# One 256-column lane and then 512 columns in the first block of a fused attention and two-layer kernel, with part of the weight scaling moved to ScalarE

## The chip, the cores and the metric

The kernel runs on one NeuronCore of a Trainium2 chip. The metric is the device time of the whole program in microseconds (us), lower is better. Engines are named as in the profile: PE is TensorE (PEld its weight loads), DVE is VectorE, ACT is ScalarE, SP is SyncE, which here only issues DMAs.

## The reference

Three stages run one after the other on fp32 data; the output of each feeds the next.

```python
s = concat([scale * q_l @ k_g.T, where(|i-j| <= 32, scale * q_l @ k_l.T, -1e9)])   # local rows
out_l = softmax(s) @ concat([v_g, v_l]);  out_g = softmax(scale * q_g @ k_all.T) @ v_all
x  = concat([out_g, out_l]) as 2176 rows x 512
h  = x @ w_in;  g = max(h, 0) + alpha * min(h, 0);  x = g @ w_out                  # layer 1, 512 -> 2048 -> 512
h  = x @ w_in2; x = (h * clip(h + 3, 0, 6) / 6) @ w_out2                            # layer 2
```

## The kernel before, in words

**Layer 1** goes over five blocks of rows (`blocks`; the first three of 512 rows, which are the columns of every matmul here). Within a block the hidden width of 2048 is cut into `NJ` = 16 chunks `j` of 128. A step computes one chunk: `h_tile` (L424) makes the chunk of h in 12 matmuls (4 chunks of the model width, three products each, since a fp32 number is split into a high and a low part), `act` applies the activation (ACT `t` L434, DVE `t` L436, ACT `g` L442, DVE `g` L443), and `LAG` = 2 steps later `y_tiles` (L455) adds g times the second weight to the four sums y, in 12 matmuls.

**The first block** needs its weights and its x while both are still being made. x comes from the local attention (`attention_steps`; scores L194, softmax L212 and L216, transposes L227, values L240), two steps of which are interleaved with each of the first four steps, and one with each later step. Four later attention steps make one pair of units. Since only the first 256 rows are there when the block starts, it has two lanes: columns 0 to 256 run chunk j at step s = j, columns 256 to 512 run chunk j at step s = j + `DELAY`, with `DELAY` = 4. So steps 0 to 3 have 12 h matmuls of 256 columns, steps 4 to 15 have 24 of them (two chunks, 256 columns each), steps 16 to 19 have 12. Before step 4 the x of the second lane is transposed (L409) and split (ACT L395, DVE L396).

**The weights** arrive as raw 64-bit words, one half chunk (128x512) at a time: a DMA (`load_raw`, L94) into one of `RAW` = 5 buffers, then `to_float32`: ACT clamps the low word in place (L109), DVE scales the high word into a tile z of `ZB` = 2 buffers (L113), DVE shifts and merges (L117), DVE merges the sign (L119). `split_w` then makes the high part on ACT (L125) and the low part on DVE (L126). There are 32 halves. The class `Weights` converts them in the order in which the steps need them: `needed(s)` counts the halves that steps up to s use, and step s converts as far as step s + `AHEAD` = 2 needs. All this is in program order for the clamp and the scaling (`here`); the rest of the order is set by a scheduler that simulates the program.

Blocks 1 to 4 use the converted weights, with 512 columns (384 and less in the last two). The weights of layer 2 are converted with the same `to_float32` during blocks 1 to 4. Layer 2 follows.

Of the kernel before, what the change touches and what calls it, by code (L numbers as in the profile page):

```python
# [12 lines left out]
U32 = mybir.dt.uint32  # L13
# [9 lines left out]
NJ = DFF // 128  # L23
# [7 lines left out]
LAG = 2  # L31
RAW = 5
EARLY = 3
AHEAD = 2
# [5 lines left out]
TB = 2  # L40
DELAY = 4
STEPS = [[2] * 4 + [1] * 16, [1] * 16, [1] * 16, [1] * 16, [0] * 16]
CONVERT = (3, 4, 5)
SPLIT = (0, 70, 70, 30, 43)
STREAM = 3
# [10 lines left out]
def fused_kernel(ctx, tc, qkE, vE, qgz, kN, vN, vgN, w1, w2, consts, out):  # L56
# [41 lines left out]

    here = tc.keep_in_program_order

    def to_float32(raw, on_dve=True):

        words = raw.bitcast(U32).rearrange("p (f two) -> p f two", two=2)
        low, high = words[:, :, 0], words[:, :, 1]
        here(nc.scalar.activation(low, low, AF.Relu, bias=quarter_sb, scale=0.9 * 2.0 ** -29))  # L109
        z = work.tile([128, 512], F32, tag="z", name="z", bufs=ZB)  # L110
        bits = z.bitcast(U32)
        if on_dve:
            here(nc.vector.tensor_scalar(out=z, in0=high.bitcast(F32), scalar1=2.0 ** -112, scalar2=None,  # L113
                                         op0=ALU.mult))
        else:
            here(nc.scalar.activation(z, high.bitcast(F32), AF.Copy, scale=2.0 ** -112))
        nc.vector.scalar_tensor_tensor(out=bits, in0=bits, scalar=3, in1=low, op0=ALU.logical_shift_left,  # L117
                                       op1=ALU.bitwise_or)
        nc.vector.scalar_tensor_tensor(out=bits, in0=high, scalar=0x80000000, in1=bits, op0=ALU.bitwise_and,  # L119
                                       op1=ALU.bitwise_or)  # L120
        return z

    def split_w(raw, wt, m):
        z = to_float32(raw)
        nc.scalar.copy(wt[:, m, 0, :], z)  # L125
        nc.vector.tensor_tensor(out=wt[:, m, 1, :], in0=z, in1=wt[:, m, 0, :].bitcast(F32), op=ALU.subtract)  # L126

    class Weights:
# [1 line left out]


        def __init__(self, src, early=False):
            self.src, self.raw, self.next, self.wt, self.got = src, {}, 0, {}, 0
            self.seq = [(j, m) for j in range(NJ) for m in range(2)]
            if early:
                self.seq.sort(key=lambda h: (h[0] + LAG * h[1], -h[1]))
# [5 lines left out]
        def fetch(self, upto):  # L142
            while self.got < min(upto, 2 * NJ):
                self.raw[self.got] = load_raw(self.src, *self.seq[self.got])
                self.got += 1

        def convert(self, halves):
            for _ in range(halves):
                k = self.next
                if k == 2 * NJ:  # L150
                    return
                self.fetch(EARLY)
                j, m = self.seq[k]
                if j not in self.wt:
                    self.wt[j] = wp.tile([128, 2, 2, 512], F32R, tag="w", name="wt", bufs=NJ)
                split_w(self.raw.pop(k), self.wt[j], m)
                self.fetch(k + EARLY + 1)
                self.next += 1

# [231 lines left out]
    width = [sum(128 if x == "g" else 256 for x in blk) for blk in blocks]  # L391
# [6 lines left out]
    def x_tiles():  # L398
        return [work.tile([128, 2, 512], F32R, tag="xt", name="xt", bufs=HP) for _ in range(HP)]

    def x_from_attention(pieces, xt, at):

        for hp in range(HP):
            t = bank("xt_ps")
            n = 0
            for piece in pieces:
                x = xo.pop(("g", hp) if piece == "g" else (*piece, hp))
                for i in range(1 if piece == "g" else 2):
                    nc.tensor.transpose(t[:, n:n + 128], x if piece == "g" else x[:, i, :], ident_sb)  # L409
                    n += 128  # L410
            split_x(t[:, :n], xt[hp][:, :, at:at + n], n)

    def active(lanes, s):
        return [(a, b, s - d) for a, b, d in lanes if 0 <= s - d < NJ]

    def h_tile(xt, wts, parts):
        ps = bank("h_ps")
# [26 lines left out]
    def y_tiles(layer, y, g, wts, parts, lanes=False):  # L446
        for a, b, j in parts:
            steps = [(w, c) for w in ((0, 0), (1, 0), (0, 1)) for c in range(len(y))]
            if j == NJ - 1:
                steps.sort(key=lambda step: step[1])  # L450
            for (wl, gl), c in steps:
                first = a == 0 and j == 0 and (wl, gl) == (0, 0)
                last = j == NJ - 1 and (wl, gl) == (0, 1) and (not lanes or b == 512)
                if layer == 0:
                    nc.tensor.matmul(y[c][:, a:b], lhsT=wts[j][:, 1, wl, 128 * c:128 * c + 128], rhs=g[:, gl, a:b],  # L455
                                     start=first, stop=last, skip_group_check=lanes)
                else:
                    nc.tensor.matmul(y[c], lhsT=g[:, gl, 128 * c:128 * c + 128], rhs=wts[j][:, 1, wl, :],
                                     start=first, stop=last)
# [22 lines left out]
    def attention_steps(n):  # L482

        for _ in range(n):
            if state["gen"] is None:
                return
            try:
                next(state["gen"])
            except StopIteration:
                state["pool"].close()  # L490
                state["gen"] = None
                if not state.get("global"):
                    state["global"] = True
                    state["pool"] = ExitStack()
                    state["gen"] = global_units(state["pool"].enter_context(tc.tile_pool(name="gatt", bufs=1)))

    def ready(pieces):
        return all((("g", hp) if x == "g" else (*x, hp)) in xo for x in pieces for hp in range(HP))
# [438 lines left out]
    W1 = Weights(w1, early=True)  # L937
# [5 lines left out]
    k = 0  # L943
    while not ready(blocks[0][:1]):
        attention_steps(1)
        k += 1
        if k in CONVERT:
            W1.convert(1)
# [3 lines left out]
    for bi in range(len(blocks)):  # L952
        n = width[bi]
        last = bi == len(blocks) - 1
        lanes = [(0, 256, 0), (256, 512, DELAY)] if bi == 0 else [(0, n, 0)]
        y = [psy.tile([128, 512], F32, tag="y", name="y_ps", bufs=4) for _ in range(NC)]
        gs, xt_next = {}, None
        end = NJ + lanes[-1][2]
        for s in range(end + LAG):
            if s < end:  # L960
                if bi == 0:
                    if s == DELAY:
                        while not ready(blocks[0][1:]):
                            attention_steps(1)
                        x_from_attention(blocks[0][1:], xt, 256)
                    W1.convert(W1.needed(s) - W1.next)
                    W1.convert(min(1, W1.needed(s + AHEAD) - W1.next))
                parts = active(lanes, s)
                gs[s] = act(0, h_tile(xt, W1.wt, parts), parts)
                if bi == 0:  # L970
                    W1.convert(W1.needed(s + AHEAD) - W1.next)
                attention_steps(STEPS[bi][s])
            if last and s == 0:
                while state["gen"] is not None:
                    attention_steps(1)
                outs_pool.close()
                later["xs"] = pool("xs")
                more = inputs(twos[0], bt)
                plan_stream()
            if s == end - 1 and not last:  # L980
                xt_next = x_tiles()
                while not ready(blocks[bi + 1]):
                    attention_steps(1)
                x_from_attention(blocks[bi + 1], xt_next, 0)
            if s >= LAG:
                y_tiles(0, y, gs.pop(s - LAG), W1.wt, active(lanes, s - LAG), len(lanes) > 1)
            done = [SPLIT[bi] * max(x - REST, 0) // (end + LAG - REST) for x in (s, s + 1)]
            for _ in range(done[1] - done[0]):
                next(second, None)
            if last and s >= 2:  # L990
                next(more, None)
        if last:
            for _ in second:
                pass
            for _ in more:
                pass
            ahead(STREAM + RAW - 2)
        for c in range(0, NC, 2):
            r = work.tile([128, 2, 512], F32, tag="g", name="ev", bufs=LAG + 1)[:, :, :n]
            nc.scalar.copy(r[:, 0, :], y[c][:, :n])  # L1000
            nc.vector.tensor_copy(r[:, 1, :], y[c + 1][:, :n])
            for i in range(2):
                nc.sync.dma_start(out=x2[bi][:, c + i, :], in_=r[:, i, :])
        xt = xt_next
# [64 lines left out]
```

## Time and profile before

| | |
|---|---|
| median of 3 runs | 840.43 us (839.70 to 842.15) |
| profiled execution, its own time | 838.92 us |
| span in the profile of that execution | 836.8 us |
| PE busy | 817.8 us (98%), 7228 matmuls |
| PEld busy | 740.3 us (88%) |
| DVE busy | 594.1 us (71%) |
| ACT busy | 415.4 us (50%) |
| granted TensorE clock, mean | 0.994 of full speed |

The profiled execution took 2.1 us more than the span, and 1.5 us less than the median of the runs. A busy PE here is PE with a matmul in its pipeline; how fast the matmuls follow each other is read from where they start. A row of a timeline gives start, duration, engine, line, tensors and count; the duration contains a tail that overlaps the next instruction.

### The profile page before, as it was taken

The numbers are of one execution on the slowest core, as the hardware profiler recorded it, in microseconds if no ns is written. First come the engines' busy times: TensorE is split into PE (matmuls) and PEld (weight loads), VectorE is DVE, ScalarE is ACT, GpSimd is POOL, SyncE is SP. The second block draws the span as 40 slices with busy tenths as digits, with TensorE's granted clock in tenths as the row PEclk, the third lists the DMA queues.
The fourth block names the chain that finished last, engine by engine and source line by source line (L and its number), as shares of the span: only waits on it lengthen the run. The fifth ranks groups of instructions, "written<-read, shape, count | busy, mean of one in ns | idle before, by whom it ended". The sixth has DMA issues, their size and how long they took to land.

```text
span 836.8 us, 18274 instructions
## 1 busy us (share of the span) xinstructions
PE 817.8 (98%) x7228; PEld 740.3 (88%) x7228; DVE 594.1 (71%) x1319; ACT 415.4 (50%) x905; POOL 0.2 (0%) x4
## 2 busy tenths in 40 slices
PE   6889999999999999989999999999999999999997
PEld 4779999888888888878899988889999999999996
DVE  4999995477878786787678847778867678854221
ACT  5876665455656554455454523434543444432222
POOL 0000000000000000000000000000000000000000
PEclk9999999999999999999999999999999999999999
DMA  9976563367768876798575555666675878788872
GB/s 334 340 267 239 181 215 119 109 210 254 272 215 296 270 253 238 256 312 297 182 263 203 166 200 190 193 208 215 201 239 199 295 255 284 243 280 262 276 255 67
DMA packets 72868, 195.70 MB, mean 234 GB/s; under 512 B 7120, under 2 KB 18384, under 8 KB 72784
## 3 DMA queue, kind: packets, MB, share of 16 engines
q1 hardware_dynamic: 72688, 194.42, 68.8%
q8 instruction: 57, 0.93, 0.4%
q14 instruction: 27, 0.22, 0.1%
q10 hardware_dynamic: 96, 0.13, 0.1%
HBM read 152.05 MB, written 42.47 MB: 232 GB/s over the span
## 4 chain that ended last, share of the span: by engine, by line
PE 86%; DVE 6%; DMA 3%; ACT 3%; issue 1%; SPq 0%; DVEq 0%; ACTq 0%
PE y_ps L455 20%; PE h_ps L424 19%; PE o_ps L859 17%; PE k_ps L776 16%; PE h_ps L928 4%; PE o_ps L714 4%; DMA raw<-in_w 2%; PE o_ps L240 1%; PE s_ps L194 1%; DVE z L117 1%; PE pt_ps L227 1%; DVE z L119 1%; DVE wt L126 1%; DVE z L113 1%; PE xt_ps L409 1%
## 5 line engine op out<-in xcount | busy, mean ns | idle before, releaser
L455 PE MATMUL y_ps<-g,wt 128*128 128x256 f32 (+2 forms) x1152 | 209.3, 331 | 3.4 <-ACT g L442 1.7
L424 PE MATMUL h_ps<-xt,wt 128*128 128x256 f32 (+2 forms) x1152 | 206.3, 329 | 1.4 <-DVE xt L396 0.9
L455 PEld LDWEIGHTS y_ps<-g,wt 128*128 128x128 f32 x1152 | 176.5, 189 | 23.0 <-ACT g L442 2.1
L424 PEld LDWEIGHTS h_ps<-xt,wt 128*128 128x128 f32 x1152 | 177.8, 190 | 18.7 <-DVE xt L396 1.1
L859 PE MATMUL o_ps<-ws,gh 128*128 128x256 f32 x784 | 139.4, 283 | 0.0
L776 PE MATMUL k_ps<-bt,ws 128*128 128x512 f32 (+1 forms) x672 | 135.1, 362 | 0.0
L776 PEld LDWEIGHTS k_ps<-bt,ws 128*128 128x128 f32 x672 | 121.2, 188 | 13.0
L859 PEld LDWEIGHTS o_ps<-ws,gh 128*128 128x128 f32 x784 | 120.8, 192 | 0.1
L859 PE MATMUL o_ps<-ws,gl 128*128 128x256 f32 x392 | 107.0, 283 | 0.0
L790 DVE TENSOR_TENSOR gl<-far,gh 128x1024 fp32r<-128x1024 f32 (+1 forms) x56 | 60.9, 1089 | 33.0 <-ACT gh L789 32.7
L789 ACT CAST gh<-far 128x1024 fp32r<-128x1024 f32 (+1 forms) x56 | 52.7, 942 | 62.8 <-PE o_ps L859 58.5
L436 DVE SCALAR_TENSOR_TENSOR t<-t,c_sb,h_ps 128x256 f32<-128x256 f32 (+2 forms) x96 | 55.2, 588 | 32.3 <-ACT t L434 32.0
L859 PEld LDWEIGHTS o_ps<-ws,gl 128*128 128x128 f32 x392 | 73.5, 192 | 0.0
L434 ACT ACTIVATE t<-h_ps 128x512 f32<-128x512 f32 (+2 forms) x84 | 42.8, 511 | 52.9 <-PE h_ps L424 51.2
L442 ACT CAST g<-t 128x512 fp32r<-128x512 f32 (+2 forms) x84 | 45.3, 539 | 43.8 <-DVE t L436 43.7
L443 DVE TENSOR_TENSOR g<-t,g 128x512 fp32r<-128x512 f32 (+2 forms) x84 | 49.2, 587 | 21.3 <-ACT g L442 18.7
L761 ACT ACTIVATE t<-far,half_sb 128x512 f32<-128x512 f32 (+1 forms) x48 | 32.1, 671 | 50.9 <-DVE far L757 49.7
L216 ACT ACTIVATE p<-p,st 128x128 f32<-128x128 f32 x128 | 49.7, 390 | 11.9 <-DVE st L212 11.9
L109 ACT ACTIVATE raw<-raw,quarter_sb 128x512 uint32<-128x512 uint32 x64 | 49.6, 775 | 3.7 <-DMA raw<-in_w 3.7
L117 DVE SCALAR_TENSOR_TENSOR z<-z,raw 128x512 uint32<-128x512 uint32 x64 | 43.7, 691 | 3.3 <-ACT raw L109 0.8
L119 DVE SCALAR_TENSOR_TENSOR z<-raw,z 128x512 uint32<-128x512 uint32 x64 | 43.6, 689 | 0.7
L928 PE MATMUL h_ps<-xt,ws 128*128 128x384 f32 x192 | 36.0, 336 | 0.0
(100 smaller groups left out, 854.8 us busy)
## 6 DMA issues: line engine op xcount, KB each, us to landing
ws<-wo SPq DMA_DIRECT2D x72, 512.0 KB, 4.2
raw<-in_w SPq DMA_DIRECT2D x64, 512.0 KB, 5.4
ws<-wi SPq DMA_DIRECT2D x64, 512.0 KB, 4.6
v_t<-in_vE SPq DMA_DIRECT2D x32, 512.0 KB, 7.1
qk_t<-in_qkE SPq DMA_DIRECT2D x32, 368.0 KB, 5.5
wi<-raw SPq DMA_DIRECT2D x16, 512.0 KB, 3.1
wi<-parts SPq DMA_DIRECT2D x16, 512.0 KB, 4.5
wo<-raw SPq DMA_DIRECT2D x16, 512.0 KB, 4.0
```

What stands on the lines that cost most here:

```text
L109: here(nc.scalar.activation(low, low, AF.Relu, bias=quarter_sb, scale=0.9 * 2.0 ** -29))
L117: nc.vector.scalar_tensor_tensor(out=bits, in0=bits, scalar=3, in1=low, op0=ALU.logical_shift_left, op1=ALU.bitwise_or)
L119: nc.vector.scalar_tensor_tensor(out=bits, in0=high, scalar=0x80000000, in1=bits, op0=ALU.bitwise_and, op1=ALU.bitwise_or)
L216: nc.scalar.activation(p[:, n, :], p[:, n, :], AF.Exp, bias=st[:, 1, n:n + 1], scale=-1.0, accum_out=st[:, 2, n:n + 1])
L424: nc.tensor.matmul(ps[:, a:b], lhsT=wts[j][:, 0, wl, 128 * c:128 * c + 128], rhs=xt[c][:, xl, a:b], start=k == 0, stop=k == 3 * NC - 1)
L436: nc.vector.scalar_tensor_tensor(out=t[:, c:d], in0=t[:, c:d], scalar=c1_sb[:, j:j + 1], in1=ps[:, c:d], op0=ALU.mult, op1=ALU.add)
L455: nc.tensor.matmul(y[c][:, a:b], lhsT=wts[j][:, 1, wl, 128 * c:128 * c + 128], rhs=g[:, gl, a:b], start=first, stop=last, skip_group_check ...
L776: nc.tensor.matmul(bank, lhsT=wt[:, wl, at:at + 128], rhs=bt[x][:, c, xl, 0:w], start=first and k == 0, stop=k == 5, skip_group_check=True)
L789: nc.scalar.copy(hi, src)
L790: nc.vector.tensor_tensor(out=lo, in0=src, in1=hi.bitcast(F32), op=ALU.subtract)
L859: mm = nc.tensor.matmul(bank, lhsT=part[:, jp, 128 * c:128 * c + 128], rhs=wo[:, jp, 256 * wl:256 * wl + 256], start=opens, stop=k == NP / ...
L928: nc.tensor.matmul(h, lhsT=wt[:, wl, 128 * c:128 * c + 128], rhs=xt[c][:, xl, 0:w], start=k == 0, stop=k == 3 * NC - 1)
```

## The change

From the ninth half on (`SCALED_ON_DVE` = 8) the scaling of the high word runs on ACT, as `AF.Copy` with a scale, and `to_float32` is cut in two: `begin_float32` (load of the raw words, clamp, scaling) is called one half ahead of `end_float32` (the two merges). The first block keeps the 20 steps, but steps 0 to 3 run columns 0 to 256 for chunks 0 to 3, steps 4 to 7 run columns 256 to 512 for the same chunks 0 to 3, and steps 8 to 19 run all 512 columns for chunks 4 to 15. `converted(s)` tells how far the conversion is to be at step s: by it steps 5 and 7 convert two halves, steps 4, 6, 8 and 9 none, steps 10 to 17 two each, 18 and 19 one each, where before steps 4 to 13 converted two each.

```diff
+SCALED_ON_DVE = 8
...
         here(nc.scalar.activation(low, low, AF.Relu, bias=quarter_sb, scale=0.9 * 2.0 ** -29))
         z = work.tile([128, 512], F32, tag="z", name="z", bufs=ZB)
         if on_dve:
             here(nc.vector.tensor_scalar(out=z, in0=high.bitcast(F32), scalar1=2.0 ** -112, scalar2=None,
                                          op0=ALU.mult))
         else:
             here(nc.scalar.activation(z, high.bitcast(F32), AF.Copy, scale=2.0 ** -112))
+        return z, low, high
...
+        def begin(self, k):
+            if k < 2 * NJ and k not in self.begun:
+                self.begun[k] = begin_float32(self.raw.pop(k), k < SCALED_ON_DVE)
...
-                split_w(self.raw.pop(k), self.wt[j], m)
+                self.begin(k)
+                if k + 1 >= SCALED_ON_DVE:
+                    self.begin(k + 1)
+                split_w(self.begun.pop(k), self.wt[j], m)
...
-    def active(lanes, s):
-        return [(a, b, s - d) for a, b, d in lanes if 0 <= s - d < NJ]
+    def active(bi, s):
+        if bi:
+            return [(0, width[bi], s)] if s < NJ else []
+        if s < DELAY:
+            return [(0, 256, s)]
+        if s < 2 * DELAY:
+            return [(256, 512, s - DELAY)]
+        return [(0, 512, s - DELAY)] if s - DELAY < NJ else []
+
+    def converted(s):
+        return s if s < DELAY else max(s - DELAY, DELAY - 1 + (min(s, 2 * DELAY) - DELAY + 1) // 2)
...
-                    W1.convert(W1.needed(s) - W1.next)
-                    W1.convert(min(1, W1.needed(s + AHEAD) - W1.next))
+                    W1.convert(W1.needed(converted(s)) - W1.next)
+                    W1.convert(min(1, W1.needed(converted(s) + AHEAD) - W1.next))
```

**PE, from the h matmuls of step 4 on.** Before, where both lanes are in every step:

```order
L424 MATMUL h_ps<-xt,wt 128x256 x24
L455 MATMUL y_ps<-g,wt 128x256 x4
L424 MATMUL h_ps<-xt,wt 128x256
L227 MATMUL pt_ps<-consts_sb,p 128x128 x8
L455 MATMUL y_ps<-g,wt 128x256 x8
L424 MATMUL h_ps<-xt,wt 128x256 x23
L455 MATMUL y_ps<-g,wt 128x256 x24
L424 MATMUL h_ps<-xt,wt 128x256 x24
```

In the changed kernel (L449 is h, L480 is y), after the first 16 h matmuls of steps 4 and 5 and 4 of y:

```order
L480 MATMUL y_ps<-g,wt 128x256 x4
L449 MATMUL h_ps<-xt,wt 128x256 x6
L241 MATMUL pt_ps<-consts_sb,p 128x128 x4
L449 MATMUL h_ps<-xt,wt 128x256 x2
L241 MATMUL pt_ps<-consts_sb,p 128x128 x4
L480 MATMUL y_ps<-g,wt 128x256 x8
L449 MATMUL h_ps<-xt,wt 128x256 x24
L208 MATMUL s_ps<-qk_t 32x128 x5
L480 MATMUL y_ps<-g,wt 128x256 x12
L208 MATMUL s_ps<-qk_t 32x128 x27
L254 MATMUL o_ps<-v_t,pt 32x64 x32
L480 MATMUL y_ps<-g,wt 128x256 x12
```

The 24 h matmuls that were one step of two lanes are now two steps of the second lane; the first h of 512 columns follows the last row shown.

**DVE, around the splitting of the second lane's x before step 4.** Before:

```order
L113 TENSOR_SCALAR z<-raw 128x512 x2
L218 TENSOR_SCALAR st<-st 128x4
L396 TENSOR_TENSOR xt<-xt_ps,xt 128x256
L117 SCALAR_TENSOR_TENSOR z<-z,raw 128x512
L218 TENSOR_SCALAR st<-st 128x4
L117 SCALAR_TENSOR_TENSOR z<-z,raw 128x512
L220 RECIPROCAL rs<-st 128x4
L396 TENSOR_TENSOR xt<-xt_ps,xt 128x256 x3
```

In the changed kernel (L410 is the splitting, L121 and L123 the two merges):

```order
L410 TENSOR_TENSOR xt<-xt_ps,xt 128x256
L121 SCALAR_TENSOR_TENSOR z<-z,raw 128x512
L410 TENSOR_TENSOR xt<-xt_ps,xt 128x256
L123 SCALAR_TENSOR_TENSOR z<-raw,z 128x512
L121 SCALAR_TENSOR_TENSOR z<-z,raw 128x512
L410 TENSOR_TENSOR xt<-xt_ps,xt 128x256 x2
```

The two scalings ahead of the first split are gone from DVE, and one merge more stands ahead of the last one.

**ACT, in two converting steps that end a cycle of attention steps.** Before:

```order
L109 ACTIVATE raw<-raw,quarter_sb 128x512
L434 ACTIVATE t<-h_ps 128x512
L442 CAST g<-t 128x512
L109 ACTIVATE raw<-raw,quarter_sb 128x512
L125 CAST wt<-z 128x512
L434 ACTIVATE t<-h_ps 128x512
L125 CAST wt<-z 128x512
L442 CAST g<-t 128x512
```

In the changed kernel (L110 clamps, L116 scales, L132 casts, L459 and L467 belong to the activation):

```order
L110 ACTIVATE raw<-raw,quarter_sb 128x512
L116 ACTIVATE z<-raw 128x512 x2
L459 ACTIVATE t<-h_ps 128x512
L132 CAST wt<-z 128x512 x2
L110 ACTIVATE raw<-raw,quarter_sb 128x512
L467 CAST g<-t 128x512
L110 ACTIVATE raw<-raw,quarter_sb 128x512
L116 ACTIVATE z<-raw 128x512 x2
```

Two scalings per step have come to ACT, in pairs: both z buffers are filled, then both are cast.

## Rows read from the trace of the kernel before

**Rows 1.** Busy time by stretch: us, PE, PEld, DVE, ACT, POOL busy (instructions), PEclk, DMA share, GB/s.
```profile
49.36:53.68 4.32, 3.13 (x24) 2.92 (x24) 4.07 (x12) 2.42 (x7) 0.00 (x0) 1.00 0.99 373
53.68:68.56 14.88, 14.77 (x117) 14.22 (x118) 14.03 (x28) 9.92 (x17) 0.00 (x0) 1.00 0.59 203
68.56:95.69 27.13, 27.04 (x330) 26.00 (x329) 25.87 (x67) 18.77 (x42) 0.00 (x0) 1.00 0.63 219
95.69:123.23 27.54, 27.35 (x330) 26.18 (x329) 26.09 (x67) 18.76 (x43) 0.00 (x0) 1.00 0.64 221
123.23:150.83 27.60, 27.60 (x448) 26.56 (x448) 17.40 (x67) 15.34 (x53) 0.00 (x0) 1.00 0.41 136
165.50:190.50 25.00, 25.00 (x241) 20.60 (x246) 17.91 (x47) 13.32 (x33) 0.00 (x0) 1.00 0.57 198
```

**Rows 2.** Chain of waits, 0 to 260 us: start, us, what.
```profile
6.79 11.16 DMA raw<-in_w
...
80.99 4.67 DMA raw<-in_w
...
133.18 1.44 PE h_ps L424 x12
...
144.79 0.59 PE xt_ps L409 x4
...
147.29 1.31 PE xt_ps L409 x12
...
160.07 2.72 PE y_ps L455 x12
```

**Rows 3.** Chain of waits, 150 us to the end: its shares by engine and line.
```profile
by line: PE y_ps L455 20.8%; PE o_ps L859 20.5%; PE h_ps L424 20.3%; PE k_ps L776 19.6%; PE h_ps L928 4.9%; PE o_ps L714 4.8%; PE o_ps L240 1.2%; PE s_ps L194 1.1%; PE pt_ps L227 1.0%; PE gs_ps L332 0.9%; PE go_ps L377 0.8%; PE xt_ps L409 0
```

**Rows 4.** Timeline of PE: where stretches begin.
```profile
53.68 0.75 PE L455 MATMUL y_ps<-g,wt 128*128 128x256 f32 x4 [1.19 <-ACT wt L125]
...
150.83 5.63 PE L424 MATMUL h_ps<-xt,wt 128*128 128x512 f32 x24
...
165.44 1.16 PE L194 MATMUL s_ps<-qk_t 64*32 64x128 f32 x64
...
190.44 1.16 PE L194 MATMUL s_ps<-qk_t 64*32 64x128 f32 x64
```

**Rows 5.** Groups by line and form, PE, 53.6 to 150.8 us: count, busy us, mean ns.
```profile
L455 PE MATMUL y_ps<-g,wt 128*128 128x256 f32 x348 | 46.5, 287 | 1.5 <-ACT wt L125 1.4
L424 PE MATMUL h_ps<-xt,wt 128*128 128x256 f32 x312 | 41.6, 285 | 0.1
```

**Rows 6.** The same view, DVE, 53.6 to 128.6 us and 165 to 240 us.
```profile
L436 DVE SCALAR_TENSOR_TENSOR t<-t,c_sb,h_ps 128x256 f32<-128x256 f32 x24 | 10.4, 476 | 0.7 <-ACT t L434 0.7
...
L436 DVE SCALAR_TENSOR_TENSOR t<-t,c_sb,h_ps 128x512 f32<-128x512 f32 x12 | 8.9, 746 | 7.7 <-ACT t L434 7.7
```

**Rows 7.** Timelines of DVE and of ACT: instructions that follow each other without a gap.
```profile
48.16 0.74 DVE L113 TENSOR_SCALAR z<-raw 128x512 f32<-128x512 f32 x2
...
50.59 1.04 DVE L396 TENSOR_TENSOR xt<-xt_ps,xt 128x256 fp32r<-128x256 f32 x3
...
67.61 0.42 DVE L113 TENSOR_SCALAR z<-raw 128x512 f32<-128x512 f32 x1
67.95 0.69 DVE L443 TENSOR_TENSOR g<-t,g 128x512 fp32r<-128x512 f32 x1
...
60.22 0.78 ACT L109 ACTIVATE raw<-raw,quarter_sb 128x512 uint32<-128x512 uint32 x1
60.89 0.60 ACT L442 CAST g<-t 128x512 fp32r<-128x512 f32 x1
61.40 0.77 ACT L109 ACTIVATE raw<-raw,quarter_sb 128x512 uint32<-128x512 uint32 x1
```

**Rows 8.** DMA issues (count, KB each, median us to landing), 53.6 to 128.6 us.
```profile
raw<-in_w SPq DMA_DIRECT2D x20, 512.0 KB, 4.3
```

**Rows 9.** Waits of the DMA queue, 49 to 130 us: us in total, times, longest.
```profile
SPq L169 <- PE s_ps L194: 7.0, 3, 5.7
```

More of the change, by code (lines that the diff above doesn't have):

```diff
@@ L99, in fused_kernel, with begin_float32 @@
     here = tc.keep_in_program_order
-    def to_float32(raw, on_dve=True):
+    def begin_float32(raw, on_dve=True):
         words = raw.bitcast(U32).rearrange("p (f two) -> p f two", two=2)
@@ L110, in to_float32 @@
         z = work.tile([128, 512], F32, tag="z", name="z", bufs=ZB)
-        bits = z.bitcast(U32)
         if on_dve:
@@ L116, in to_float32, with end_float32 @@
             here(nc.scalar.activation(z, high.bitcast(F32), AF.Copy, scale=2.0 ** -112))
+        return z, low, high
+    def end_float32(z, low, high):
+        bits = z.bitcast(U32)
         nc.vector.scalar_tensor_tensor(out=bits, in0=bits, scalar=3, in1=low, op0=ALU.logical_shift_left,
@@ L121, in to_float32, with split_w @@
         return z
-    def split_w(raw, wt, m):
-        z = to_float32(raw)
+    def to_float32(raw):
+        return end_float32(*begin_float32(raw))
+    def split_w(begun, wt, m):
+        z = end_float32(*begun)
         nc.scalar.copy(wt[:, m, 0, :], z)
@@ L132, in __init__ @@
         def __init__(self, src, early=False):
-            self.src, self.raw, self.next, self.wt, self.got = src, {}, 0, {}, 0
+            self.src, self.raw, self.next, self.wt, self.got, self.begun = src, {}, 0, {}, 0, {}
             self.seq = [(j, m) for j in range(NJ) for m in range(2)]
@@ L954, in fused_kernel @@
         last = bi == len(blocks) - 1
-        lanes = [(0, 256, 0), (256, 512, DELAY)] if bi == 0 else [(0, n, 0)]
         y = [psy.tile([128, 512], F32, tag="y", name="y_ps", bufs=4) for _ in range(NC)]
         gs, xt_next = {}, None
-        end = NJ + lanes[-1][2]
+        end = NJ + (DELAY if bi == 0 else 0)
         for s in range(end + LAG):
@@ L965, in fused_kernel @@
                         x_from_attention(blocks[0][1:], xt, 256)
-                    W1.convert(W1.needed(s) - W1.next)
-                    W1.convert(min(1, W1.needed(s + AHEAD) - W1.next))
-                parts = active(lanes, s)
+                    W1.convert(W1.needed(converted(s)) - W1.next)
+                    W1.convert(min(1, W1.needed(converted(s) + AHEAD) - W1.next))
+                parts = active(bi, s)
                 gs[s] = act(0, h_tile(xt, W1.wt, parts), parts)
                 if bi == 0:
-                    W1.convert(W1.needed(s + AHEAD) - W1.next)
+                    W1.convert(W1.needed(converted(s) + AHEAD) - W1.next)
                 attention_steps(STEPS[bi][s])
@@ L985, in fused_kernel @@
             if s >= LAG:
-                y_tiles(0, y, gs.pop(s - LAG), W1.wt, active(lanes, s - LAG), len(lanes) > 1)
+                y_tiles(0, y, gs.pop(s - LAG), W1.wt, active(bi, s - LAG), bi == 0)
             done = [SPLIT[bi] * max(x - REST, 0) // (end + LAG - REST) for x in (s, s + 1)]
```

## The prediction

> **What bounds the kernel now.** I read the chain of waits first. From 150 us to the end it is matmuls, by line: nearly nothing else holds a share of it [rows 3], so from the start of block 1, at 150.83 us [rows 4], the time is matmul work, and what the change can move is how early that point comes. I then cut the time before it into stretches [rows 1]. From 53.68 us, where the two lanes are both running, PE is busy to 99%, but so are its weight loads (26.00 of 27.13 us), and DVE is busy 25.87 of 27.13 us. In block 1, with 512 columns, a stretch of the same length in steps (four steps and one pair of attention units, from one score group at 165.44 to the next at 190.44 [rows 4]) takes 25.00 us, with the weight loads at 20.60 and DVE at 17.91. So in the first block four steps of two lanes cost 27.13 and 27.54 us, and four steps of one 512-wide lane 25.00 us, for the same products.
>
> **Two prices make up that difference.** A run of 12 matmuls of 256 columns takes 1.44 us on the chain, 0.120 us each; 12 of 512 columns take 2.72 us, 0.2267 us each [rows 2]. Two narrow ones thus cost 0.2400 where one wide one costs 0.2267: 0.0133 us saved per pair. The rest is waiting. One pair of attention units costs PE 25.00 − 8 × 2.72 = 3.24 us in block 1, transitions included, and four steps of two lanes would cost 4 × 48 × 0.120 + 3.24 = 26.28 us without any wait; they take 0.85 and 1.26 us more.
>
> **The sum, part by part.** I count from 53.68 us to 150.83 us, 97.15 us.
>
> *Floor before.* 348 + 312 = 660 matmuls of 256 columns are left [rows 5]: 79.2 us. Four pairs of attention units: 12.96 us. The 16 transposes of the next block's x: 0.59 + 1.31 = 1.90 us [rows 2]. Together 94.06 us, so 3.1 us of the stretch is waiting.
>
> *Floor after.* From the same point (the 24 h matmuls of steps 4 and 5 done, in both kernels) there are 24 h matmuls of 256 columns for steps 6 and 7, 12 of y for the first lane's chunk 3 and 48 of y for the second lane's chunks 0 to 3: 84 × 0.120 = 10.08 us. Chunks 4 to 15 take 12 × 24 = 288 wide ones: 65.29 us. With 12.96 and 1.90 that is 90.2 us. The wide matmuls are worth 288 × 0.0133 = **3.8 us**; they are on the path, since PE is the bound in the stretch.
>
> Here a rule differs from the rows. The rows say 0.120 and 0.2267 us. The Trainium skill's page "TensorE: Matmul & The Clock Gate", section "Back-to-back issue gap", gives an isolated gap of columns / 2.4 + 2.5 ns, which makes 109 and 216 ns; by it (an estimate) a pair would save 2.5 ns and the 288 of them 0.7 us. The sum goes by the rows, where every matmul has its own weight load.
>
> *Waits after.* 3.1 us of waiting is there to win; how much of it goes depends on DVE and ACT. DVE: a scaling costs 0.34 us (67.61 to 67.95 [rows 7]), eight per four steps: 2.7 us less. The activation's DVE step is now one 512-wide instruction of mean 746 ns instead of two of 476 ns [rows 6], which overlap their tails by about 0.09 us; estimated from both means, 0.13 us per step less, 0.5 us per four. DVE's 25.87 us per four steps become 22.6, against 25.0 of PE: 90%, where it was 95% of the time it took. ACT: a scaling on ACT stands in no row. The cast with contiguous operands takes 0.51 us (60.89 to 61.40), the clamp, which reads the same raw tile with the same stride, 0.67 us (60.22 to 60.89) [rows 7]; I take 0.67, the nearest, and 0.51 as the other end. Eight per four steps add 5.4 us (4.1): ACT's 18.77 us become 24.1 (22.9), of 25.0. That is no bound yet, but it is close. Two things cover it. Conversion runs two steps ahead of use, and y comes two steps after its h: between them stand y, h, y, h, 4 × 2.72 = 10.9 us. And only eight of the twelve wide steps convert two halves. I leave 1.3 us of the 3.1 us waiting, **1.8 us** won; the ends are 3.1 (no wait left) and −2.0 (rival 1).
>
> *The start, steps 4 and 5.* Before, both lanes' h ran as soon as x came; now only the second lane's 12 matmuls can, and each fourth of them needs its own split of x. DVE loses two scalings ahead of the first split (0.67 us), and has one merge more ahead of the last split. The splits take 0.33 us each (1.04 for three with the last tail [rows 7]) and the merges as much as g, about 0.6: 4 × 0.33 + 3 × 0.6 = 3.1 us from 48.2 us, so the last split ends at 51.4 and 18 matmuls follow it at most: 53.5 us, against 53.68. I count this as **0**, from 1 us earlier (the splits come sooner) to 1 us later (a cast is late on ACT, behind the exponentials). In steps 6 and 7 PE has h matmuls of 2.9 us, one y of 1.44 us and attention before it needs the g of step 4, which DVE finishes some 4 us after that step's h: no wait is priced.
>
> *Edits at nothing.* Scaling one half ahead takes one more raw tile into use early; the DMA of 512 KB lands in 4.3 us [rows 8] and there are five buffers for about two halves per 6.25 us, so the transfer stays hidden; without that cover see rival 2. Fewer PE instructions, the same DMAs. After the block nothing is moved, and an earlier start of block 1 is carried to the end by the matmul chain.
>
> **Sum: 3.8 + 1.8 + 0 = 5.6 us.** The profiled execution, 838.92 us, would become 833.3; the median of the runs shown is 1.5 us above it, so I predict 840.43 − 5.6 = **834.8 us**, 0.7% faster. About 0.3% (2.5 us) can be told from no change.
>
> **Rivals.**
>
> *1. ACT and DVE take the bound together.* With two z buffers, both are scaled on ACT, merged twice on DVE, cast on ACT and subtracted on DVE before the next pair may start; ACT at 24.1 of 25.0 us has no room for waits in this round. For it: DVE was 95% busy and made PE wait; ACT's instructions now stand in the same round. Against it: ACT idles a third of the stretch now, and two steps of lead stand in between. If four converting steps still took the 27.3 us that they take now (mean of 27.13 and 27.54), the eight would cost 2 × 2.34 = 4.7 us instead of 1.3: 838.2 us; half of it gives 836.5. The Trainium skill's page "ScalarE: Activation LUTs", section "Rules for kernel authors", speaks against this edit: a multiplication belongs on VectorE. The rows of before show the clamp and the casts on ACT alone, not the same multiplication on both.
>
> *2. The raw words come too late (slower).* ACT takes its work in order, so a clamp that waits for its DMA holds up the casts and the activation behind it. A buffer is now held from landing through up to two halves (6.2 us) and its own clamp and merges (about 1.9 us); five buffers at 3.1 us per half give 15.6 us, which leaves 7.5 us for the transfer. For it: the chain ran through a raw transfer at 80.99 us, and one took 11.16 us at the start [rows 2]; loads of the next attention units wait 7.0 us in the DMA queue for PE's scores [rows 9], with raw loads behind them. Against it: 4.3 us is the median, at a DMA share of about 0.6 [rows 1]. If they took 11.2 us, a half would take (11.2 + 8.1) / 5 = 3.9 us, a step 7.7 instead of 6.25, and nine steps 13 us more: 834.8 + 13 = 847.8 us. It decides from about 7.5 us per transfer on; below 10 us the result is between.
>
> *3. The wide matmuls save little.* If the 0.120 us of the narrow ones in this block comes from what runs beside them and not from their width, the wide ones would meet it too and the 3.8 us go: 838.6 us. By the gap of the page named above it would be 837.9 us. Against it: 1.44 us for 12 is seen near the block's end, where DVE has nothing to convert any more [rows 2], and 2.72 us in block 1, where it is converting again.
>
> **Chances.** Forecast 0.68; rival 1 0.18; rival 2 0.08; rival 3 0.04; 0.02 for more than the forecast. Under 837.9 us lie the forecast, the better case and half of rival 1: 0.79, given as 0.8 for faster. The other half and rival 3 make 0.13, given as 0.12 for the same. Rival 2 is slower: 0.08. The range: at the low end no wait and a start 0.5 us earlier (834.8 − 1.8) and 1 us of spread between runs, 832; at the high end rival 1 in full with the same 1 us, 839.2. It leaves out rival 2 and what lies beyond the low end.
>
> **What would show it.** Right: block 1's first h starts near 145 us in the span; the 12-matmul runs of 512 columns in the first block take 2.72 us; DVE's share in four wide steps is near 90%, and so is ACT's, and the scaling on ACT takes 0.5 to 0.7 us. Rival 1: PE waits for `g` or `wt` by several us between 75 and 135 us. Rival 2: ACT's clamp waits for the raw DMA by more than 5 us in total, and the DMAs land later than 7 us. Rival 3: no waits, but fewer us saved. The prediction is wrong if block 1 starts later than 149 us, or earlier than 142 us.

## The result, and the profile after

The changed kernel takes 831.94 us (median of 5 runs, 831.57 to 833.49), against 840.31 us for the kernel before (5 runs): ratio 0.9904, 95% interval 0.9887 to 0.9921, so 8.4 us less, with 6.6 to 9.5 us inside the interval. Two later comparisons on other occasions gave 7.8 us (ratio 0.9909) and 7.3 us (0.9910). The forecast was 834.8 us, with a range from 832.0; the time lies just under that end.

| | before | after |
|---|---|---|
| median, us | 840.31 | 831.94 |
| profiled execution, its own time | 838.92 | 831.75 |
| span | 836.8 | 829.9 |
| PE matmuls | 7228 | 6940 |
| first h matmul of step 4 (in the profile) | 49.36 | 49.73 |
| block 1 starts | 150.83 | 144.02 |
| from there to the end of the span | 685.97 | 685.88 |

The last row says that all of the gain was made before block 1: 6.8 us of the 6.9 us by which the spans differ. This is the timeline of PE after, at the places that answer to [rows 4]; L449 is h, L208 the scores, L480 y:

```profile
49.73 0.85 PE L449 MATMUL h_ps<-xt,wt 128*128 128x256 f32 x5 [1.25 <-DVE xt L410]
50.89 1.57 PE L449 MATMUL h_ps<-xt,wt 128*128 128x256 f32 x11 [0.30 <-DVE xt L410]
52.30 0.64 PE L480 MATMUL y_ps<-g,wt 128*128 128x256 f32 x4
...
81.86 1.16 PE L208 MATMUL s_ps<-qk_t 64*32 64x128 f32 x64
...
106.85 1.16 PE L208 MATMUL s_ps<-qk_t 64*32 64x128 f32 x64
...
131.84 1.16 PE L208 MATMUL s_ps<-qk_t 64*32 64x128 f32 x64
...
144.02 5.61 PE L449 MATMUL h_ps<-xt,wt 128*128 128x512 f32 x24
```

From one score group to the next are four wide steps and one pair of attention units: 24.99 us, twice. That is what the same work takes in block 1 before (25.00 us), where nothing is converted for this layer. After the 0.30 us at 50.89 the view shows no idle time of PE in the stretch. The busy times of the stretches [rows 1], after (us, PE, PEld, DVE, ACT, POOL, clock, DMA share, GB/s):

```profile
52.30:81.86 29.56, 29.56 (x299) 26.07 (x297) 24.47 (x61) 23.99 (x56) 0.00 (x0) 1.00 0.68 224
81.86:106.85 24.99, 24.99 (x234) 20.59 (x233) 22.63 (x55) 22.77 (x50) 0.00 (x0) 1.00 0.68 236
106.85:131.84 24.99, 24.99 (x233) 20.59 (x232) 22.18 (x53) 20.46 (x46) 0.00 (x0) 1.00 0.60 205
131.84:144.02 12.18, 12.18 (x182) 10.35 (x181) 7.57 (x29) 7.48 (x24) 0.00 (x0) 1.00 0.49 162
```

In the first of these two cycles DVE has 22.63 us of work and ACT 22.77 us, where they had 25.87 and 18.77 us in a longer one (27.13 us). The weight loads fell from 26.00 to 20.59 us. Who waited for whom between 49 and 145 us (us in total, times, longest):

```profile
ACT wt L132 <- DVE z L123: 7.2, 9, 1.5
DVE z L121 <- ACT z L116: 6.0, 11, 1.4
...
PE h_ps L449 <- DVE xt L410: 1.5, 2, 1.2
```

ACT and DVE wait for each other in the conversion, 13 us together, and no wait of PE is put down to it: the two waits of PE are those at the start of step 4. Handovers as such are not new: before, ACT's cast waited 10.1 us for DVE's merges in the same stretch.

### The profile page after: what moved, and what is told of

It reads as the page before. It is cut to its first block, busy times and chain, and to the rows that moved or that the text cites. A ratio compares the mean times of both kernels' runs of the same rounds, so it can differ in the third digit from the quotient of the medians.

```text
span 829.9 us, 17685 instructions
## 1 busy us (share of the span) xinstructions
PE 812.1 (98%) x6940; PEld 724.3 (87%) x6940; DVE 585.1 (70%) x1283; ACT 427.4 (51%) x929; POOL 0.2 (0%) x4
## 4 chain that ended last, share of the span: by engine, by line
PE 92%; ACT 3%; DVE 2%; DMA 2%; issue 0%; SPq 0%; ACTq 0%; DVEq 0%
PE y_ps L480 22%; PE h_ps L449 22%; PE o_ps L884 17%; PE k_ps L801 16%; PE h_ps L953 4%; PE o_ps L739 4%; DMA qk_t<-in_qkE 2%; PE s_ps L208 2%; PE o_ps L254 2%; PE pt_ps L241 1%; ACT p L230 1%; PE xt_ps L423 1%; PE gs_ps L346 1%; PE go_ps L391 1%; DVE z L121 0%; PE gpt_ps L373 0%
## 5 line engine op out<-in xcount | busy, mean ns | idle before, releaser
L480 PE MATMUL y_ps<-g,wt 128*128 128x512 f32 (+2 forms) x1008 | 206.3, 353 | 1.7 <-ACT g L467 1.7
L449 PE MATMUL h_ps<-xt,wt 128*128 128x512 f32 (+2 forms) x1008 | 204.3, 352 | 2.3 <-DVE xt L410 1.5
L449 PEld LDWEIGHTS h_ps<-xt,wt 128*128 128x128 f32 x1008 | 170.1, 191 | 24.7 <-DVE xt L410 2.4
L480 PEld LDWEIGHTS y_ps<-g,wt 128*128 128x128 f32 x1008 | 167.5, 189 | 25.6 <-ACT g L467 2.1
L461 DVE SCALAR_TENSOR_TENSOR t<-t,c_sb,h_ps 128x512 f32<-128x512 f32 (+2 forms) x84 | 53.5, 641 | 27.9 <-ACT t L459 27.7
L459 ACT ACTIVATE t<-h_ps 128x512 f32<-128x512 f32 (+2 forms) x84 | 42.6, 512 | 45.0 <-PE h_ps L449 43.9
L467 ACT CAST g<-t 128x512 fp32r<-128x512 f32 (+2 forms) x84 | 45.2, 538 | 35.3 <-DVE t L461 35.0
L121 DVE SCALAR_TENSOR_TENSOR z<-z,raw 128x512 uint32<-128x512 uint32 x64 | 43.6, 688 | 9.3 <-ACT z L116 6.0
L110 ACT ACTIVATE raw<-raw,quarter_sb 128x512 uint32<-128x512 uint32 x64 | 49.3, 772 | 1.2 <-DMA raw<-in_w 1.2
L123 DVE SCALAR_TENSOR_TENSOR z<-raw,z 128x512 uint32<-128x512 uint32 x64 | 43.4, 688 | 0.7
```

The source lines that it names most:

```text
L449: nc.tensor.matmul(ps[:, a:b], lhsT=wts[j][:, 0, wl, 128 * c:128 * c + 128], rhs=xt[c][:, xl, a:b], start=k == 0, stop=k == 3 * NC - 1)
L461: nc.vector.scalar_tensor_tensor(out=t[:, c:d], in0=t[:, c:d], scalar=c1_sb[:, j:j + 1], in1=ps[:, c:d], op0=ALU.mult, op1=ALU.add)
L467: nc.scalar.copy(g[:, 0, a:b], t[:, a:b])
```

## The experiments

Each ratio is that to the kernel before, timed on the same occasion. Theory A is that of the prediction: 3.8 us from wide matmuls, and about 3 us of waits that the relief of DVE and the slower pace take away. The rivals are B (the scaling's move does all of it) and C (lanes and pace do all of it), and for the later runs D, E and F, as the expectations say.

**The changed kernel again.**

> The changed kernel once more, beside the others on the same chip. All theories: 832 us, between 831 and 834, block 1's first h matmul at 144 us of the span (150.8 before).

832.03 us, ratio 0.9909 (0.9895 to 0.9922).

**The scaling back on DVE.**

```diff
-SCALED_ON_DVE = 8
+SCALED_ON_DVE = 64
```

> The lanes and the conversion pace of the changed kernel, but every scaling back on DVE and none one half ahead. Theory A (3.8 us from wide matmuls, about 3 us from waits that DVE's relief and the slower pace take away): the 3.8 us stay; DVE has 25.3 us of work per four converting steps against 25.0 of PE, so 1 to 3 us of waits come back: 833 to 835.5 us. Theory B (all of the gain is the scaling leaving DVE): 838 us or more. Theory C (all of it is lanes and pace): 832 us.

833.02 us, ratio 0.9921 (0.9907 to 0.9934): 6.8 us of the 7.8 us are there without the scaling's move. The 1.0 us between this and the changed kernel is within the two intervals. B falls; C (832 us) is not excluded. The price that A gave for the waits was at the edge: I had counted 25.3 us of DVE work in four converting steps, and these 25 us of the experiment hold less (columns as above):

```profile
85.00:110.00 25.00, 25.00 (x187) 20.04 (x189) 22.70 (x48) 16.42 (x39) 0.00 (x0) 1.00 0.53 186
110.00:135.00 25.00, 25.00 (x220) 20.02 (x216) 23.87 (x60) 17.13 (x40) 0.00 (x0) 1.00 0.62 225
```

With DVE at 91% and 95%, the chain of waits is still matmuls alone from 60 to 149 us. The timeline of PE says the same, where step 4 and block 1 start:

```profile
50.15 2.30 PE L449 MATMUL h_ps<-xt,wt 128*128 128x256 f32 x17 [0.81 <-DVE xt L410]
...
143.89 5.18 PE L449 MATMUL h_ps<-xt,wt 128*128 128x512 f32 x22
```

Between them lie 93.74 us, no more than in the changed kernel (94.29). So for this stretch the new lanes and the spread of the conversions over the steps to 19 are enough together, without the move; no run had one of the two without the other and with the scaling on DVE. What this profile loses, it loses later: 686.9 us from block 1 to its end (685.9 in the changed kernel), with a wait of PE for DVE's activation at 150.99 us (0.6 us).

**The scaling's move alone, with two lanes and the old pace.**

```diff
-            return [(0, 256, s)]
...
+        return [(a, b, s - d) for a, b, d in [(0, 256, 0), (256, 512, DELAY)] if 0 <= s - d < NJ]
...
     def converted(s):
-        return s if s < DELAY else max(s - DELAY, DELAY - 1 + (min(s, 2 * DELAY) - DELAY + 1) // 2)
+        return s
```

> The two lanes and the conversion pace of before, with only the scaling moved to ACT from the ninth half on, one half ahead. Theory A: PE's floor in the stretch stays 94.1 us, so at most the 3.1 us of waits go: 837 to 839 us, block 1 at 147.5 to 149.5 us. Theory B: 832 to 834 us. Theory C: 840 us, no change.

837.40 us, ratio 0.9969 (0.9957 to 0.9980): 2.4 us, as A has it. The timeline of PE, where step 4 and block 1 start:

```profile
49.08 2.65 PE L443 MATMUL h_ps<-xt,wt 128*128 128x256 f32 x20 [1.25 <-DVE xt L410]
...
148.21 5.63 PE L443 MATMUL h_ps<-xt,wt 128*128 128x512 f32 x24
```

99.13 us lie between, against 101.47 before and 94.29 in the changed kernel. The matmuls are those of before, so what the scaling's move, begun one half ahead, took away is waits. C falls for the old order: it had said 840 us. By medians the two halves of the change add up to more than the whole (6.8 + 2.4 against 7.8 us). The likely reading is that each removes waits that the other would have removed, but 1.4 us is no more than the intervals of three ratios allow.

**The changed kernel with its wide matmuls cut in two.**

```diff
+    def halves_of(bi, parts):
+        return [(c, min(c + 256, b), j) for a, b, j in parts for c in range(a, b, 256)] if bi == 0 else parts
...
-                gs[s] = act(0, h_tile(xt, W1.wt, parts), parts)
+                gs[s] = act(0, h_tile(xt, W1.wt, halves_of(bi, parts)), parts)
...
-                y_tiles(0, y, gs.pop(s - LAG), W1.wt, active(bi, s - LAG), bi == 0)
+                y_tiles(0, y, gs.pop(s - LAG), W1.wt, halves_of(bi, active(bi, s - LAG)), bi == 0)
```

> The changed kernel with each 512-wide h and y product of the first block issued as two of 256 columns (288 more matmuls, same sums; the activation stays 512 wide). Theory A: 288 x 0.0133 = 3.8 us slower than the changed kernel, 835.8 us, spacing of the narrow matmuls 0.120 us, hardly any waits. Theory B: no slower than the changed kernel, 832 us, since PE would use up waits.

835.87 us, ratio 0.9951 (0.9938 to 0.9963), 3.84 us more than the changed kernel on the same chip, and the two intervals do not meet. Its chain of waits is matmuls only from 60 to 150 us, as the changed kernel's is; two of its pieces (start, us, what):

```profile
89.17 2.88 PE h_ps L452 x24
92.05 2.88 PE y_ps L483 x24
```

24 narrow matmuls take 2.88 us where 12 wide ones take 2.72. Its stretch from step 4 to block 1 was 97.75 us (51.10 to 148.85), 3.46 us more than the changed kernel's. So the width is a term by itself, and it is about half of the gain.

**No half begun early.**

```diff
                 self.begin(k)
-                if k + 1 >= SCALED_ON_DVE:
-                    self.begin(k + 1)
```

> The changed kernel without the early start of the next half: the scaling is on ACT from the ninth half on, but each half is begun only when it is converted. Theory A (the conversion runs two steps ahead of PE and its own latency is covered): 832 to 833 us, no new wait of PE. Rival D (the handover from ACT to DVE has to be hidden by starting early): DVE's merge waits for ACT's scaling grow from 6 us to well over 10 us and PE waits for weights, 834 us or more.

834.96 us, ratio 0.9949 (0.9936 to 0.9962), about 3 us slower than the changed kernel's 0.9909. D was right about the time, though not about where to see it: DVE's wait for ACT's scaling only grew from 6.0 to 7.2 us. The chain of waits shows it. In the changed kernel it is matmuls from 52.46 us on; here, between 83 and 139 us, it does not run through PE at all. A piece of it (start, us, what; pieces of under 0.05 us between these are left out):

```profile
102.13 0.69 DVE z L121
102.82 0.61 DVE wt L133
103.46 0.70 ACT z L116
104.18 0.69 DVE z L121
104.87 0.60 DVE wt L133
105.48 0.60 DVE z L123
106.08 0.67 DVE t L459
106.78 0.62 ACT g L465
107.39 0.68 ACT raw L110
```

This is rival 1: merge, subtract, scale, merge, subtract, merge, activation, cast, clamp, one after the other, from engine to engine. PE waits 1.2 us at 113.43 us for the DVE part of an activation. The edit "one half ahead" of the change is what keeps that round off the path. Without it the scaling on ACT is worse than on DVE: the interval here (0.9936 to 0.9962) lies above that with every scaling on DVE (0.9907 to 0.9934).

**The old pace with the new lanes.**

```diff
     def converted(s):
-        return s if s < DELAY else max(s - DELAY, DELAY - 1 + (min(s, 2 * DELAY) - DELAY + 1) // 2)
+        return s
```

> The changed kernel with the conversion pace of before (two halves in each of the steps 4 to 13, not spread to step 19). Theory A (PE has only one narrow chunk in steps 4 to 7, so conversions there delay the activation that y waits for): DVE has about 5 us of work per step against 3.7 us of PE there, some 1 to 4 us of waits, 833 to 836 us. Rival E (the pace does not matter, since y comes two steps later): 832 us.

835.98 us, ratio 0.9958 (0.9945 to 0.9970), 4 us slower than the changed kernel. E falls, but A's place was wrong: steps 4 to 7 show no wait for y. The loss is in one cycle, 107.03 to 135.79 us, which takes 28.76 us instead of 25.0. Waits between 49 and 150 us, and the chain that leads to it:

```profile
ACT raw L110 <- DMA raw<-in_w: 5.9, 6, 2.4
...
PE o_ps L254 <- DVE t L461: 2.1, 1, 2.1
```

```profile
98.39 3.54 DMA raw<-in_w
...
101.96 0.78 ACT raw L110
102.74 0.47 ACT t L459
...
108.88 0.69 DVE z L121
109.57 0.67 DVE t L461
...
110.29 1.10 PE o_ps L254 x64
```

ACT's clamp waits for raw words (5.9 us in all; in the changed kernel no such wait stands in this stretch), the activation's first step stands behind it, and 8 us after that clamp PE waits 2.1 us for an activation on DVE. That is rival 2's mechanism in part, in a kernel that was not the changed one. Its second sign is missing: a raw transfer lands in 4.4 us (median, 52 to 145 us; 4.7 in the changed kernel), and the DMA queue waits 55.0 us for DVE's merges to give a buffer back. The 8 us behind the clamp are ACT and DVE work, as in rival 1; which of the two started it stays open.

The wait is not all of the loss in the cycle, 3.8 us. Right behind it the granted clock of PE was 0.61 on average, that is, partly at the lower of its two levels, 1.2 GHz (columns as above):

```profile
111.32:115.75 4.43, 4.43 (x18) 3.49 (x13) 4.32 (x8) 2.97 (x6) 0.00 (x0) 0.61 0.75 253
```

From the y of this step to the next h there are 4.43 us, against 2.85 us in the changed kernel (108.97 to 111.82, clock 1.00): 1.6 us more. So here a wait of 2.1 us cost PE 3.7 us.

**How many halves keep their scaling on DVE.**

```diff
-SCALED_ON_DVE = 8
+SCALED_ON_DVE = 4     # 0, 10, 12, 16
```

> Scaling on ACT from the fifth half on instead of the ninth. DVE is full before step 4 and ACT nearly (9.2 us of 10 between 40 and 50 us before). If DVE sets the start of step 4: up to 1 us earlier, 831 us. If ACT, behind its exponentials, sets it: 832 to 833 us.

> All scalings of the first layer's weights on ACT, all one half ahead. If DVE sets the start of the first block: 830 to 831 us. If ACT sets it: 833 us or more.

> Scaling on ACT from the eleventh half on instead of the ninth, so that the two scalings beside the splitting of the second lane's x go back to DVE. If ACT sets the start of step 4 (theory F, from the runs with four and with none on DVE, which started later): first h matmul of step 4 near 48.5 us instead of 49.7, then no wait: 831 us. If the start is noise between executions: 832 us.

> The same from the thirteenth half on. Theory F: as with ten, 831 us, since steps 4 to 9 convert few halves and DVE has room there. Otherwise 832 us.

> The same from the seventeenth half on, so that DVE keeps the scaling until about step 10. Theory F: 831 to 832 us; more than 832.5 if DVE's lead in the wide steps is needed.

> The changed kernel again, on the chip of the three above: 832 us, the mark that they have to beat.

| halves scaled on DVE | median, us | ratio, 95% | step 4 starts | to block 1 |
|---|---|---|---|---|
| 0 | 834.61 | 0.9945 (0.9931 to 0.9958) | 52.66 | 93.14 |
| 4 | 834.24 | 0.9940 (0.9927 to 0.9954) | 50.96 | 94.03 |
| 8, the change | 832.44 | 0.9910 (0.9897 to 0.9922) | 50.96 | 94.26 |
| 10 | 833.29 | 0.9918 (0.9904 to 0.9932) | 49.95 | 95.43 |
| 12 | 831.96 | 0.9903 (0.9889 to 0.9918) | 49.75 | 94.07 |
| 16 | 832.25 | 0.9909 (0.9895 to 0.9922) | 49.66 | 95.27 |

The last two columns are from one profile each, in us; the rows with 0 and 4 were timed on another occasion than the others, so the ratios are to be compared. From 8 to 16 nothing can be told apart; fewer than 8 costs 0.3%, some 2.5 us, and the intervals don't meet that of the change. Why is not shown. With four, 1.0 us is lost before block 1 against the first profile of the change (144.99 against 144.02) and 1.5 us behind it, 1.2 us of that in one wait of PE for DVE's activation at 426.32 us. With none on DVE, step 4 starts latest and what follows is shortest (timeline of PE):

```profile
52.66 1.09 PE L449 MATMUL h_ps<-xt,wt 128*128 128x256 f32 x5 [0.47 <-DVE xt L410]
```

so in that profile the loss is in the start of the block, though the granted clock (0.88 from 38 to 52.66 us) has a part in it. Theory F (ten and more on DVE start step 4 a microsecond earlier, 831 us) is not borne out: their starts are within 0.2 us of that of the first profile, and the change itself has been seen to start at 49.73, at 49.83 and, in the last profile, at 50.96 us:

```profile
50.96 0.86 PE L449 MATMUL h_ps<-xt,wt 128*128 128x256 f32 x5 [1.48 <-DVE xt L410]
```

The same program thus starts this step 1.2 us apart between executions. The clock goes with it: between 38 us and the start it was 1.00 in the first two profiles and 0.87 in the last. There the chain of waits runs through h matmuls of 256 columns, 2.27 us for 11 of them instead of 1.32, in a stretch at the lower level, 1.2 GHz (the chain, then the busy times):

```profile
42.34 2.27 PE h_ps L449 x11
```

```profile
42.00:44.00 2.00, 2.00 (x10) 2.00 (x11) 2.00 (x8) 0.91 (x3) 0.00 (x0) 0.50 0.82 328
```

The 95.43 us of the row with 10 have the same reason: after an idle time of 2.18 us PE had a clock of 0.70 from 49.95 to 54.40 us. No version here beats the change by more than the runs scatter.

## Why the prediction was right or wrong

**What bounds the kernel: right.** From the start of block 1 both traces take the same time to 0.1 us, and the chain is matmuls.

**The wide matmuls, 3.8 us: right.** The kernel with narrow ones loses 3.84 us by medians, 3.46 us in its stretch (one profile). By the gap that the Trainium skill's page "TensorE: Matmul & The Clock Gate", section "Back-to-back issue gap", gives, the loss would have been 0.7 us (an estimate); the runs show the rows' price. Rival 3 is out.

**The waits, 1.8 us of 3.1 won: too little.** From 52.30 us the changed kernel has 92 narrow matmuls left (11.04 us), and 65.29, 12.96 and 1.90 us as in the sum: 91.19 us. It took 91.72, so 0.5 us of waiting is left where I left 1.3. The shares behind it were right for DVE (22.6 us forecast, 22.63 and 22.18 measured); ACT, forecast at 22.9 to 24.1, had 22.77 in one cycle and 20.46 in the other. But the reason that I gave is not what the runs show. I had priced the waits by DVE's relief, from 95% to 90%. With every scaling back on DVE, at 91% and 95%, the same count leaves 0.6 us (from 50.15 us on, 108 narrow matmuls and the rest as above, 93.11 of 93.74 us). So the new lanes with the slower pace remove these waits without the relief; that the 1.8 us came out as near as they did is in part luck. The move takes waits away in the old order (2.3 us in the stretch). Two smaller things also spoke for less than 1.3. The scaling on ACT costs 0.57 us (49.11 to 49.68), not 0.67 (timeline and groups of ACT after):

```profile
49.11 0.66 ACT L116 ACTIVATE z<-raw 128x512 f32<-128x512 f32 x1
49.68 0.35 ACT L409 CAST xt<-xt_ps 128x256 fp32r<-128x256 f32 x1
```

```profile
L110 ACT ACTIVATE raw<-raw,quarter_sb 128x512 uint32<-128x512 uint32 x21 | 16.2, 773 | 0.0
L116 ACT ACTIVATE z<-raw 128x512 f32<-128x512 f32 x22 | 14.0, 662 | 0.0
```

And the 13 us that ACT and DVE wait for each other are followed by no wait of PE in the wide steps. That the two steps of lead cover them is argued, not shown: no run shortened the lead alone. One bound of that term was also wrong: by the prediction's own 4.7 us of waits, the end for rival 1 is 3.1 − 4.7 = −1.6, not −2.0; the 838.2 us uses the right one.

**The start, 0: right in size.** In the first profile the common point (24 h matmuls of steps 4 and 5 done) comes, by count, 0.4 us earlier than before (52.30 + 8 × 0.12 = 53.26 against 53.68), but the scatter of that start is 1.2 us, so no gain or loss is shown.

**The sum.** By the profile it is 3.8 + 2.6 + 0.4 = 6.8 us, and block 1 starts 6.8 us earlier. That the two agree is no check, since the waits are what the count leaves over. Forecast were 5.6; the step that failed is "I leave 1.3 us of the 3.1 us waiting": 0.5 us were left. What the medians show beyond it, up to 8.4 us in the first comparison and 7.3 in the last, lies within the scatter of the runs of both kernels, which I had put at 1 us: those of the kernel before lie between 838.41 and 842.15 us.

**Rivals 1 and 2** did not come in the changed kernel. The cycles of 24.99 us exclude the first, and ACT's clamps wait 1.2 us for DMAs in the whole program. Rival 1 is real, though: it appears when the early start is taken back. With the old pace the clamps' waits of rival 2 appear, but not its late transfers. The rule of the Trainium skill's page "ScalarE: Activation LUTs", section "Rules for kernel authors", that a multiplication belongs on VectorE, spoke against the move. The runs bear it out in part: with the scaling back on DVE the kernel was 1.0 us slower, not faster, though the intervals meet; in the old order the move gained 2.4 us; without the early start it lost.

## What to carry to other kernels

Price a matmul that can be wide or cut in two from two stretches of the same trace. Here, where every matmul has its own weight load, a cut costs 0.0133 us, and a cut that only serves the order of the work is paid on the path. Where two engines prepare operands for a third, spread the preparation over all steps that consume them, and begin the next item on the first engine before the last is done: here the two were then at 90% beside PE, and PE had no wait for them. Before moving an operation between engines, try the better order with the operation where it is: here 6.8 of 7.8 us were there without the move.

## What the runs showed of the hardware that was not expected

ACT reads strided words in 773 ns in the clamp (a bias from a tile, written back in place with the same stride) and in 662 ns in the scaling (a constant scale alone, written to a contiguous tile), 512 columns both. The cast, with contiguous operands and no bias, took 620 ns. The Trainium skill's page "ScalarE: Activation LUTs", section "What ACT_TABLE_LOAD costs", gives 186 ns + 0.833 ns per column with constants alone, which makes 613 ns for 512 columns (an estimate), and 93 ns more for a per-partition operand. The trace agrees on the cast. Between the clamp and the scaling it shows 111 ns and between the scaling and the cast 42 ns; how much of these is the operand, the strided read or the strided write, no run here separates.
